# Block attention and a gated MLP on one core: the sums of x's quarters in two places, and all steps in another order

## The chip, the cores and the metric

The kernel runs on one NeuronCore of a Trainium2 chip. The metric is the device time of one execution in microseconds (us); several executions are taken and their median is given. The engines are TensorE (PE, matmuls), VectorE (DVE), ScalarE (ACT), GpSimd (POOL) and SyncE (SP), which here only issues DMA transfers. Each engine works through its own list of instructions in order and waits on semaphores for the others.

## The reference

Eight batches, eight heads, 576 tokens, head size 64. Attention is computed inside chunks of 64 tokens; its output, put together over the heads, is x (8 x 576 x 512), and x goes through a gated MLP:

```python
scores = scale * matmul(q_c, k_c.T);  attn = softmax(scores)      # per chunk of 64 tokens
x = matmul(attn, v_c) put back to [batch, 576, 512]
h = x @ w_in;  h = gelu_tanh(h);  u, v = h[..., :512], h[..., 512:]
v_n = (v - mean) / sqrt(var + 1e-6) * g_ln                          # over the 512 features
v_s = einsum('ts,bsd->btd', w_sg, v_n) + b_sg[None, :, None]        # over the 576 tokens
out = x + (u * v_s) @ w_out
```

All is in float32.

## The kernel before

Everything lies with features on partitions and tokens along the free axis. A product of two float32 matrices is made of three products of their high and low parts (`hi`, `lo`), so PE runs three matmuls for each. From batch 2 on, the products with w_in's half for u and with w_out are not eight quarter products but seven (a Strassen-Winograd scheme, products 1, 5, 2, 6, 3, 7, 4); the sums of weight quarters that it needs (factors) are made once, kept in DRAM and loaded again for every batch into a ring of four places of 512 KB. The sums of x's quarters that products 5, 7, 6 and 4 need are made anew in every batch, by `x_quarters`.

The program is a list of steps. Each step is a generator that issues some instructions and yields; the string `ORDER` (line 53 on) names, token by token, which step issues its next piece, and the loop at the end of the program just follows it. So the order of the instructions on every engine, on SP's queue of transfers too, is written out there. A token is a letter and a number: `v61` is unit 1 of batch 6. The letters that matter here:

- `A`: load of a tile of q, k and v (two tiles make the pair that `P` and `Q` work on; from tile 5 on five transfers each). `S`, `P`: the scores of one or two tiles and their softmax. `T`: transposition of the softmax's result (from tile 5 on DVE transposes blocks, line 556, and ACT copies them, lines 560 and 566). `O`, `Q`: attention output of one or two tiles (line 601) and `keep`, which copies it out of PSUM: the high part xh on ACT (line 629), the low part xl on DVE (631), x itself, xf, on ACT (633), and for the last tokens of a batch two more copies on ACT (640).
- `W`, `w`, `X`, `x`, `Y`: preparation of the weights. `E`, `B`, `C`, `K`: preparation of the factors. `f`: the load of the next factor into the ring (line 311).
- `v`: one of five units of v: 12 matmuls of 128x512 (line 654), gelu on ACT into hs (658), the layer norm's statistics on DVE (662 to 665), a power on POOL (667), the norm on DVE (669), its scaling on ACT (675) and the low part on DVE (677).
- `z`: `x_quarters`, one of four: a sum on POOL (763), its high part by a copy on ACT (766) and its low part on DVE (768), both into xt. `q`: a quarter product of u (781), copied by ACT (790) or added by DVE (793), with a gelu on ACT (795). The results stand in u2, of which there is one tile: a batch's first write to it waits until the tile's last reader of the batch before is done.
- `s`: a unit of the product with w_sg (731). `p`: a quarter product with w_out (849), added up on DVE (854) and stored by SP (860); the stores of products 3, 7 and 4 read u2.

PSUM holds two kinds of buffers: one pair of banks for the scores (`banks`), and three buffers of two banks (`pm`) that all other matmuls take in turn. A buffer comes free when the copy or gelu that reads it last is done. Running quarter products keep a buffer over several steps.

In `x_quarters` before, every sum is written to one place, the quarter (1, 0) of u2:

```python
t = quarter_of(u2[b], 1, 0)
a, c = {5: (x(0, 1), x(0, 0)), 7: (x(1, 1), x(0, 1)), 6: (t, x(0, 0)), 4: (x(1, 0), t)}[p]
X_SUM[p].tensor_tensor(t, a, c, op=ALU.add if p == 6 else ALU.subtract)
```

So a sum waits until DVE has read the one before it for its low part.

Of the kernel before, what the change touches and what calls it, by code (L numbers as in the profile page):

```python
# [74 lines left out]
v24 z24 P16 f6 q22 P14 q26 v24 v24 z24 P14 v24 q23 f7 z24 q26 P14 v24 v24 P14 v24 f8 q23 s20 v24 v24 q22 T15 q23 T14
T15 P16 s21 T15 T15 s20 T15 T15 P16 s20 T14 T14 s20 T14 s20 q27 T14 T14 s21 s21 Q14 f9 q27 P16 q24 A18 s21 P16 Q14 s22
s21 Q14 f10 A19 q27 P16 q24 P16 Q14 s23 s22 T17 s22 s22 T17 T16 T17 s22 T17 s22 T17 T17 s22 p21 T16 s23 T16 s23 s23 p25
s23 f11 T16 s23 s23 p21 p21 p22 f12 s23 T16 T16 p21 p21 p26 f13 p25 p25 p22 P18 p25 p22 f14 p26 p23 P18 P18 p27 f15 p23
P18 v30 p27 p23 f16 P18 p27 P18 P18 p24 v30 v30 Q16 v30 f17 p24 v30 T19 p24 v31 Q16 v30 A20 T18 T19 Q16 v30 T19 T19 v30
# [5 lines left out]
P23 f27 p35 p35 p33 f28 p36 p32 p37 P23 p32 f29 p33 P23 O22 f30 p37 p33 v40 P23 O22 p37 A26 O22 P23 O22 O22 P23 O22 p34
v40 v40 v41 f31 p34 v40 O22 p34 T24 O22 v40 O22 v40 T24 T23 v42 v40 v41 v40 T24 v41 T24 T24 v41 T24 T23 v41 v41 q41 v42
z45 v41 v42 v43 f32 q41 v41 z45 v42 T23 z45 v42 T23 T23 v42 z47 T23 v44 v43 v42 v43 v42 z47 z47 q45 v43 v44 z46 v44 q42
v44 v43 f33 z46 v43 q45 v44 z46 v43 P25 v44 f34 z44 q42 v44 q46 v43 q42 z44 P25 q43 f35 q46 v44 z44 q47 v44 v44 f36 q43
v44 v44 q43 s40 f37 q47 P25 q47 P25 Q23 s40 P25 s40 s41 A27 Q23 P25 s40 Q23 P25 s40 A28 Q23 q44 s41 T26 s41 T25 s42 f38
q44 s41 T26 s41 T26 T26 T26 T26 T25 s43 s42 T25 T25 s42 s42 s42 T25 s42 T25 s42 p41 s43 s43 s43 s43 p45 f39 s43 s43 p41  # L90
p41 P27 s43 f40 p41 p42 p41 p45 p45 P27 p46 f41 p45 p42 p43 f42 p46 p42 P27 p47 f43 p43 P27 p43 v50 p47 f44 P27 p47 P27
P27 p44 v50 v50 Q25 v50 f45 p44 v50 v50 p44 q51 Q25 A29 T27 T28 v50 v51 Q25 T27 T27 v50 T27 f46 Q25 A30 T27 v52 T27 z55
q51 v51 T28 v51 z55 v51 v53 T28 z55 v51 T28 T28 v51 z57 T28 v52 v51 v52 v51 Q27 v53 v52 z57 v53 v52 q55 A31 Q27 z57 v53
z56 Q27 P29 q55 v52 f47 v53 Q27 A32 v53 z56 q52 P29 v53 z56 v52 f48 q52 Q27 q56 z54 Q27 P29 q52 z54 v53 q53 f49 q56 z54
v52 S31 f50 q53 q57 P29 S31 P29 s50 f51 q57 q53 P29 q57 S31 P29 s51 S31 T30 s50 T29 s50 T30 S31 s50 S31 q54 T30 s51 T30
T30 s50 s51 T29 T31 s52 f52 T30 T29 s51 T29 s51 T29 T29 Q29 q54 s52 s53 A33 Q29 s52 s52 Q29 T31 T31 A34 s52 Q29 s52 p51
T31 s52 T31 s53 T31 s53 s53 p55 f53 s53 s53 s53 p51 p51 p52 f54 s53 p51 P32 p51 f55 p55 p55 p52 p56 p55 p52 P32 O31 f56
p53 p56 A35 O31 O31 P32 O31 p57 O31 p53 f57 O31 p53 v60 P32 p57 f58 p57 P32 P32 p54 v60 P32 v60 v61 v60 f59 p54 v60 v60
O31 p54 O31 T33 v60 T32 T33 q61 v60 v61 T33 v61 T33 v62 T33 f60 v61 T33 v61 v61 O31 T32 v61 z65 q61 v61 v63 v62 z65 v62
T32 z65 T32 T32 v62 T32 z67 v64 v63 v63 v62 z67 v62 v63 v62 z67 v63 P34 v64 v63 z66 v64 v63 q65 v62 z66 q62 v64 f61 q65  # L100
z66 v64 v64 z64 q66 f62 q62 v64 v63 q62 q63 v64 f63 v64 q66 P34 v64 Q32 f64 z64 q63 v64 q67 z64 q63 v64 Q32 P34 s60 f65
q67 Q32 q67 Q32 q64 s60 s60 P34 s61 f66 s60 P34 s60 P34 q64 P34 s62 s61 s61 T34 T35 s61 T34 s61 s63 T34 s62 T34 T34 s62
s62 s62 T34 s62 T35 s62 T35 T35 T35 p61 T35 s63 s63 s63 s63 p65 f67 s63 s63 p61 p61 p62 s63 f68 p61 p61 p66 p65 f69 p65
p62 p65 p62 p63 f70 p66 p67 f71 p63 p63 Q34 f72 p67 p67 p64 Q34 Q34 v70 f73 p64 Q34 p64 v71 v70 v70 v70 v70 v70 v72 z75
# [884 lines left out]
```

## Time and profile before

| | |
|---|---|
| time, median of 3 runs | 504.89 us (504.75 to 506.33) |
| the profiled execution | 504.94 us, its span 503.2 us |
| granted clock of PE | 0.999 of full speed over the span |
| busy in the span | PE 483.1 us, DVE 390.4, ACT 342.9, POOL 120.6 |
| instructions | 12519 |

The profile follows one execution. A row of the timeline gives the start in us from the span's start, the duration, the engine, the line of the program, the operation, what it writes and what it reads, the shapes and the count; in brackets stands how long the engine had been idle before it and what ended that. Matmuls overlap, so their ends are modelled.

### The profile page before, as it was taken

What the parts mean: (1) busy time and instruction counts of PE and PEld (TensorE: products, weight loads), DVE (VectorE), ACT (ScalarE), POOL (GpSimd) and SP (SyncE); (2) the same over time, 40 slices, a digit from 0 to 9 for tenths busy, and PEclk for the clock granted to TensorE, in tenths of its full rate; (3) what the DMA queues carried; (4) which work ended last, traced back from release to release, by engine and by line L of the source; (5) the groups of instructions that cost most, each with busy time, mean ns of one, the idle gap of its engine ahead of it and who ended that gap; (6) DMA issues with size and microseconds to landing.
All of it is one profiled execution on the core that took longest, in us unless ns stands there. A gap on an engine that the chain in (4) does not pass through costs nothing.

```text
span 503.2 us, 12519 instructions
## 1 busy us (share of the span) xinstructions
PE 483.1 (96%) x5112; PEld 441.1 (88%) x5112; DVE 390.4 (78%) x678; ACT 342.9 (68%) x645; POOL 120.6 (24%) x106
## 2 busy tenths in 40 slices
PE   3989999999999999999999999999899999999996
PEld 2767899899998789988999889997899889998996
DVE  7888969977855887878769678777859787867555
ACT  5789898833765689659984777649995678625320
POOL 0112000001491351116310362014320260206200
PEclk9999999999999999999999999999999999999999
DMA  8969010387265983897877846487929915192515
GB/s 293 386 181 284 22 44 22 107 246 238 88 229 173 326 258 126 221 292 205 249 214 221 238 136 207 136 295 231 289 70 278 304 63 210 42 326 89 184 57 205
DMA packets 70189, 97.98 MB, mean 195 GB/s; under 512 B 36978, under 2 KB 50290, under 8 KB 70132
## 3 DMA queue, kind: packets, MB, share of 16 engines
q1 hardware_dynamic: 70132, 97.18, 61.5%
q8 instruction: 40, 0.66, 0.5%
q14 instruction: 17, 0.14, 0.1%
HBM read 80.38 MB, written 16.78 MB: 193 GB/s over the span
## 4 chain that ended last, share of the span: by engine, by line
PE 76%; DVE 8%; ACT 7%; DMA 6%; POOL 2%; issue 1%; SPq 0%; POOLq 0%; DVEq 0%; ACTq 0%
PE pm L731 22%; PE pm L654 14%; PE pm L849 11%; PE pm L781 10%; PE pm L703 5%; PE pm L907 4%; PE pm L601 3%; PE banks L502 3%; DMA out_dram<-u 2%; PE pm L246 2%; DMA qkv_t<-qkv 2%; ACT L658 1%; ACT ptT L566 1%; POOL u L763 1%; DMA ring<-factors 1%
## 5 line engine op out<-in xcount | busy, mean ns | idle before, releaser
L731 PE MATMUL pm<-wsg,v 128*128 128x288 f32 x768 | 108.0, 296 | 0.2 <-ACT u L795 0.2
L731 PEld LDWEIGHTS pm<-wsg,v 128*128 128x128 f32 x768 | 103.9, 189 | 0.7 <-ACT u L795 0.3
L539 POOL TENSOR_TENSOR pt<-pt,den 128x1024 f32<-128x1024 f32 (+1 forms) x15 | 27.4, 1825 | 134.0 <-DVE den L536 98.5
L667 POOL TENSOR_TENSOR sm<-sm,neg_half 128x1 f32<-128x1 f32 x36 | 28.5, 794 | 109.0 <-DVE sm L665 107.6
L654 PE MATMUL pm<-wv_h,xl 128*128 128x512 f32 x128 | 51.7, 404 | 2.7 <-DVE xl L631 1.1
L566 ACT COPY ptT<-blocks 32x256 f32<-32x256 f32 x124 | 50.1, 404 | 2.2
L654 PE MATMUL pm<-wv_h,xh 128*128 128x512 f32 x128 | 50.6, 395 | 0.0
L654 PE MATMUL pm<-wv_l,xh 128*128 128x512 f32 x128 | 50.6, 395 | 0.0
L781 PE MATMUL pm<-xt,ring 128*128 128x288 f32 x288 | 44.0, 300 | 1.2 <-ACT xt L766 0.6
L781 PEld LDWEIGHTS pm<-xt,ring 128*128 128x128 f32 x288 | 39.5, 188 | 3.0 <-DVE xt L768 1.3
L849 PE MATMUL pm<-gh,ring 128*128 128x288 f32 x192 | 40.9, 297 | 0.0
L662 DVE BATCH_NORM_STATS2 sm<-hs 128x6 f32<-128x512 f32 x36 | 24.7, 690 | 20.4 <-ACT hs L658 20.2
L781 PE MATMUL pm<-xh,ring 128*128 128x288 f32 x144 | 31.9, 297 | 1.9 <-ACT xf L633 1.2
L654 PEld LDWEIGHTS pm<-wv_h,xl 128*128 128x128 f32 x128 | 24.0, 188 | 9.3 <-DVE xl L631 1.6
L849 PE MATMUL pm<-tv,ring 128*128 128x288 f32 x216 | 31.9, 297 | 0.2 <-DMA ring<-factors 0.2
L677 DVE SCALAR_TENSOR_TENSOR v<-hs,sm,v 128x512 fp32r<-128x512 f32 x32 | 28.1, 881 | 5.0 <-ACT v L675 4.8
L849 PEld LDWEIGHTS pm<-gh,ring 128*128 128x128 f32 x192 | 31.5, 188 | 0.3
L737 DVE TENSOR_TENSOR u<-pm,u 128x576 f32<-128x576 f32 x24 | 18.0, 751 | 17.0 <-PE pm L731 14.2
L849 PEld LDWEIGHTS pm<-tv,ring 128*128 128x128 f32 x216 | 29.7, 188 | 1.1 <-issue 0.6
L654 PEld LDWEIGHTS pm<-wv_h,xh 128*128 128x128 f32 x128 | 24.0, 188 | 5.8
L675 ACT ACTIVATE v<-hs,sm 128x512 fp32r<-128x512 f32 x32 | 22.9, 721 | 8.2 <-DVE hs L669 4.7
L654 PEld LDWEIGHTS pm<-wv_l,xh 128*128 128x128 f32 x128 | 24.1, 188 | 4.8
(175 smaller groups left out, 1151.6 us busy)
## 6 DMA issues: line engine op xcount, KB each, us to landing
ring<-factors SPq DMA_DIRECT2D x84, 512.0 KB, 4.4
qkv_t<-qkv SPq DMA_DIRECT2D x32, 512.0 KB, 5.1
qkv_t<-qkv SPq DMA_DIRECT2D x124, 64.0 KB, 4.3
out_dram<-u SPq DMA_DIRECT2D x18, 288.0 KB, 5.7
factors<-fac SPq DMA_DIRECT2D x16, 256.0 KB, 2.8
out_dram<-ot SPq DMA_DIRECT2D x14, 288.0 KB, 2.3
qkv_t<-qkv SPq DMA_DIRECT2D x3, 768.0 KB, 11.3
wsg<-w_in SPq DMA_DIRECT2D x4, 512.0 KB, 4.0
```

The lines of the kernel that those rows point to most:

```text
L539: eng.tensor_tensor(pt, pt, den.unsqueeze(2).broadcast_to([P, n, D]), op=ALU.mult)
L566: nc.scalar.copy(ptT[q[1 - a], :, a, :], blocks[q[a], :, 1 - a, :])
L654: nc.tensor.matmul(pv, a[:, kt, tok], c[:, kt, :], start=(i == 0), stop=(i == 11))
L662: nc.vector.bn_stats(st, h)
L667: nc.gpsimd.tensor_tensor(rs, rs, neg_half, op=ALU.pow)
L675: nc.scalar.mul(hi, h, rs)
L677: nc.vector.scalar_tensor_tensor(lo, h, rs, hi.bitcast(F32), op0=ALU.mult, op1=ALU.subtract)
L703: nc.tensor.matmul(pm[:, j, :HS], a[:, kt, dc], c[:, kt, j * HS : (j + 1) * HS], start=(i == 0), stop=(i == 11))
L731: nc.tensor.matmul(pm[:, j, :HS], a[:, dc], c[:, m, j * HS : (j + 1) * HS], start=(i == 0), stop=(i == len(ops) - 1))
L781: nc.tensor.matmul(pm[:, e, :HS], a[:, k, e * P : (e + 1) * P], c[:, k, :], start=starts and i == 0, stop=i == len(ops) - 1, skip_group_ch ...
L849: nc.tensor.matmul(pm[:, e, :HS], a[:, k, e * P : (e + 1) * P], c[:, k, :], start=starts and i == 0, stop=i == len(ops) - 1, skip_group_ch ...
L907: nc.tensor.matmul(pm[:, j, :HS], a[:, kt, ec], c[:, kt, j * HS : (j + 1) * HS], start=(i == 0), stop=(i == len(ops) - 1),)
```

## The change

It has two parts. In `x_quarters` the sums stand in two places of u2 by turns: those for products 5 and 6 in the quarter (0, 1), those for 7 and 4 in the quarter (1, 0). The numbers that are summed are the same: 6 is still made from 7's sum, and 4 from 6's.

```diff
         begin_u(b)
-        t = quarter_of(u2[b], 1, 0)
-        a, c = {5: (x(0, 1), x(0, 0)), 7: (x(1, 1), x(0, 1)), 6: (t, x(0, 0)), 4: (x(1, 0), t)}[p]
+
+        t1, t2 = quarter_of(u2[b], 1, 0), quarter_of(u2[b], 0, 1)
+        t, a, c = {
+            5: (t2, x(0, 1), x(0, 0)), 7: (t1, x(1, 1), x(0, 1)), 6: (t2, t1, x(0, 0)), 4: (t1, x(1, 0), t2)
+        }[p]
         X_SUM[p].tensor_tensor(t, a, c, op=ALU.add if p == 6 else ALU.subtract)
```

The other part is the string `ORDER`: the same 1641 tokens, the same steps, in another order over the whole program. Its last line, as an example:

```diff
-f82 p71 p71 p76 f83 p75 p75 p75 p73 p76 p77 p73 p73 p74 p77 p72 p77 p77 p72 p74 p74
+f82 p75 p71 p76 f83 p71 p75 p73 p76 p72 p75 p77 p72 p73 p73 p74 p77 p77 p77 p74 p74
```

Lines after `x_quarters` carry a number higher by three in the changed kernel (763 is 766 there, 781 is 784, 854 is 857). On PE the moves that matter here are these: attention output O0 before the weight steps w2 and w3; in batch 4 O22 behind v41 (it stood before v40); in batch 5 Q27 behind q53 (it stood behind the fourth unit v53, ahead of q52); in batch 6 O31 behind v61 (it stood before the last output products of batch 5); v70 ahead of the last output product of batch 6, p64 (it stood behind it). Three places show what that does to the lists of the other engines.

First, POOL in batch 7 (u_5848 and u_5873 are batch 7's u2, xf is x, line 667 is the power of the layer norm; the brackets name what an instruction waits for). Before:

```order
L667 TENSOR_TENSOR sm<-sm,neg_half 128x1 [waits DVE_49]
L763 TENSOR_TENSOR u_5848<-xf 128x2x288 [waits DMAHW2_49,DMAHW6_49,DMAHW0_49,Activation_49]
L667 TENSOR_TENSOR sm<-sm,neg_half 128x1 [waits DVE_49]
L763 TENSOR_TENSOR u_5848<-xf 128x2x288 [waits DVE_49]
L667 TENSOR_TENSOR sm<-sm,neg_half 128x1 [waits DVE_49]
L763 TENSOR_TENSOR u_5848<-u_5848,xf 128x2x288 [waits DVE_49]
L667 TENSOR_TENSOR sm<-sm,neg_half 128x1 [waits DVE_49]
L763 TENSOR_TENSOR u_5848<-xf,u_5848 128x2x288 [waits DVE_49]
```

and with the change:

```order
L667 TENSOR_TENSOR sm<-sm,neg_half 128x1 [waits DVE_49,Pool_49] x2
L766 TENSOR_TENSOR u_5873<-xf 128x2x288 [waits DMAHW2_49,DMAHW6_49,DMAHW0_49,Activation_49]
L766 TENSOR_TENSOR u_5873<-xf 128x2x288
L667 TENSOR_TENSOR sm<-sm,neg_half 128x1 [waits DVE_49,Pool_49]
L766 TENSOR_TENSOR u_5873<-u_5873,xf 128x2x288 [waits DVE_49,Pool_49]
L667 TENSOR_TENSOR sm<-sm,neg_half 128x1 [waits DVE_49]
L766 TENSOR_TENSOR u_5873<-xf,u_5873 128x2x288 [waits DVE_49,Activation_49,Pool_49]
```

The second sum follows the first with no instruction between and no wait of its own; the third and fourth still wait for DVE.

Second, ACT in batch 6, around the copies of O31 (tile 31 holds the last 64 tokens of batch 6 and the first 64 of batch 7, so `keep` copies it in two parts). Before, with pm_5076 the PSUM buffer of O31, pm_5137 that of v60 and pm_5174 that of v61:

```order
L629 CAST xh_4555<-pm_5076 128x4x64
L633 COPY xf_4554<-pm_5076 128x4x64
L629 CAST xh_5118<-pm_5076 128x4x64
L531 ACT_TABLE_LOAD
L531 ACTIVATE pt_5051<-pt_5051 128x1024
L658 ACT_TABLE_LOAD
L658 ACTIVATE hs_5150<-pm_5137 128x512
L633 COPY xf_5117<-pm_5076 128x4x64
L640 CAST xodd_0_4629<-xh_5118 128x4x64
L675 ACTIVATE v_5200<-hs_5150,sm_5172 128x512
L560 COPY ptT_5199<-blocks_5197 128x512
L658 ACTIVATE hs_5187<-pm_5174 128x512
```

and with the change, with pm_5143 that of v61, pm_5169 that of O31 and pm_5188 that of q61:

```order
L658 ACTIVATE hs_5156<-pm_5143 128x512
L629 CAST xh_4670<-pm_5169 128x4x64
L566 COPY ptT_5166<-blocks_5164 32x8x32 x3
L633 COPY xf_4669<-pm_5169 128x4x64
L629 CAST xh_5233<-pm_5169 128x4x64
L566 COPY ptT_5166<-blocks_5164 32x8x32
L793 COPY u2_5244<-pm_5188 128x2x288
L633 COPY xf_5232<-pm_5169 128x4x64
L640 CAST xodd_0_4737<-xh_5233 128x4x64
L640 CAST xodd_1_4738<-xl_5234 128x4x64
L769 CAST xt_2263<-u2_5244 128x576
L675 ACTIVATE v_5167<-hs_5156,sm_5209 128x512
```

Before, three of O31's six copies stand ahead of v60's gelu, two directly behind it, and one further on; with the change all six stand behind v61's gelu and ahead of v62's, which is the row after those shown.

Third, DVE at the very end of the program, the additions of the last output products (ot is product 2's, the last row is product 4's). Before:

```order
L834 TENSOR_TENSOR tv<-u_5848,tv 128x576
L854 TENSOR_TENSOR u_5848<-pm,xf 128x2x288
L854 TENSOR_TENSOR u_5848<-pm,u_5848 128x2x288
L854 TENSOR_TENSOR u_5848<-pm,kept 128x2x288
L854 TENSOR_TENSOR ot<-pm,kept 128x576
L854 TENSOR_TENSOR u_5848<-pm,xf 128x2x288
L854 TENSOR_TENSOR u_5848<-pm,u_5848 128x2x288
```

and with the change:

```order
L857 TENSOR_TENSOR u_5873<-pm,xf 128x2x288
L857 TENSOR_TENSOR ot<-pm,kept 128x576
L837 TENSOR_TENSOR tv<-u_5873,tv 128x576
L857 TENSOR_TENSOR u_5873<-pm,u_5873 128x2x288
L857 TENSOR_TENSOR u_5873<-pm,kept 128x2x288
L857 TENSOR_TENSOR u_5873<-pm,xf 128x2x288
L857 TENSOR_TENSOR u_5873<-pm,u_5873 128x2x288
```

The addition into ot moved from behind product 7's to ahead of product 3's.

## Rows read from the trace of the kernel before

**Rows 1.** The page, section 1: busy time of each engine, share, instructions.

```profile
PE 483.1 (96%) x5112; PEld 441.1 (88%) x5112; DVE 390.4 (78%) x678; ACT 342.9 (68%) x645; POOL 120.6 (24%) x106
```

**Rows 2.** Timeline of PE, whole span: the longer idle stretches, and what ended each.

```profile
7.72 1.97 PE L493 MATMUL pm<-qkv_t 64*64 64x64 f32 x32 [7.72 <-DMA qkv_t<-qkv]
...
28.93 0.63 PE L549 MATMUL banks<-ident,pt 128*128 128x128 f32 x4 [0.87 <-DVE pt L539]
...
30.23 1.15 PE L582 MATMUL banks<-ptT,qkv_t 64*64 64x64 f32 x32 [0.68 <-ACT xf L622]
...
185.41 0.38 PE L781 MATMUL pm<-xh,ring 128*128 128x288 f32 x1 [0.72 <-ACT u L790]
...
227.09 0.50 PE L654 MATMUL pm<-wv_h,xl 128*128 128x512 f32 x1 [1.12 <-DVE xl L631]
...
280.26 0.50 PE L654 MATMUL pm<-wv_h,xl 128*128 128x512 f32 x1 [0.43 <-ACT hs L658]
...
342.54 0.50 PE L654 MATMUL pm<-wv_h,xl 128*128 128x512 f32 x1 [0.60 <-ACT xf L633]
...
353.60 0.40 PE L781 MATMUL pm<-xh,ring 128*128 128x288 f32 x1 [1.22 <-ACT xf L633]
...
395.87 0.50 PE L654 MATMUL pm<-wv_h,xl 128*128 128x512 f32 x1 [0.43 <-ACT hs L658]
...
465.07 0.40 PE L781 MATMUL pm<-xt,ring 128*128 128x288 f32 x1 [0.57 <-ACT xt L766]
...
465.87 1.73 PE L781 MATMUL pm<-xt,ring 128*128 128x288 f32 x11 [0.39 <-DVE xt L768]
```

**Rows 3.** Timeline of batch 7's sums, all engines, 455 to 468 us.

```profile
455.80 1.68 POOL L763 TENSOR_TENSOR u<-xf 128x576 f32<-128x576 f32 x1 [1.55 <-DMA out_dram<-u]
...
458.22 0.76 DVE L768 TENSOR_TENSOR xt<-u,xt 128x576 fp32r<-128x576 f32 x1 [1.75 <-ACT xt L766]
...
459.06 1.88 POOL L763 TENSOR_TENSOR u<-xf 128x576 f32<-128x576 f32 x1 [1.07 <-DVE xt L768]
...
461.17 1.75 PE L781 MATMUL pm<-xt,ring 128*128 128x288 f32 x12
...
462.89 1.42 POOL L763 TENSOR_TENSOR u<-u,xf 128x576 f32<-128x576 f32 x1 [1.00 <-DVE xt L768]
...
463.34 1.53 DVE L677 SCALAR_TENSOR_TENSOR v<-hs,sm,v 128x512 fp32r<-128x512 f32 x1
```

**Rows 4.** Timeline of DVE's last additions, 495 us to the end.

```profile
497.64 0.75 DVE L854 TENSOR_TENSOR ot<-pm,kept 128x576 f32<-128x576 f32 x1
498.31 0.75 DVE L854 TENSOR_TENSOR u<-pm,xf 128x576 f32<-128x576 f32 x1
...
499.16 0.76 DVE L854 TENSOR_TENSOR u<-pm,u 128x576 f32<-128x576 f32 x1
```

**Rows 5.** Groups of ACT by line and shape: busy us, mean ns | idle before, releasers.

```profile
L566 ACT COPY ptT<-blocks 32x256 f32<-32x256 f32 x124 | 50.1, 404 | 2.2
...
L658 ACT ACTIVATE hs<-pm 128x512 f32<-128x512 f32 x36 | 21.5, 596 | 8.7 <-PE pm L654 6.2 <-issue 1.6 <-DVE v L677 0.7
...
L766 ACT CAST xt<-u 128x576 fp32r<-128x576 f32 x24 | 16.1, 672 | 10.1 <-POOL u L763 9.9
...
L633 ACT COPY xf<-pm 128x256 f32<-128x256 f32 x6 | 2.2, 373 | 5.5 <-DVE u L854 3.2 <-DVE xl L631 2.3
```

**Rows 6.** Timeline of PE, 385 to 404 us: O31, q61, v62, v63 begin.

```profile
386.96 0.69 PE L601 MATMUL pm<-ptT,qkv_t 64*64 64x64 f32 x32
...
398.77 0.30 PE L781 MATMUL pm<-xh,ring 128*128 128x288 f32 x1
...
400.36 0.39 PE L654 MATMUL pm<-wv_h,xl 128*128 128x512 f32 x1
...
403.15 0.40 PE L654 MATMUL pm<-wv_h,xl 128*128 128x512 f32 x1
```

**Rows 7.** Timeline of SP: the first loads into the ring.

```profile
179.50 8.10 SPq L311 DMA_DIRECT2D ring<-factors  x5
```

More of the change, by code (lines that the diff above doesn't have):

```diff
@@ L75 @@
[L75 to L79, printed above, removed]
@@ L85 @@
[L85 to L89, printed above, removed]
@@ L90 @@
[L90 to L104, printed above, removed]
@@ new lines @@
+T14 T14 P16 T14 s21 T14 T15 z24 T15 T15 T15 q23 T15 s20 q27 s20 s21 P16 s21 Q14 f9 q27 s20 P16 s21 q24 A18 Q14 s20 Q14
+s22 f10 q27 P16 s21 A19 P16 Q14 q24 s23 s22 T17 s22 T16 T17 s22 T17 s22 T17 s22 T17 T17 p21 T16 s23 T16 s22 s23 s23 p25
+s23 f11 T16 s23 s23 p21 p21 p22 f12 s23 T16 T16 p21 p26 p21 f13 p25 p25 p22 P18 p25 p22 f14 p26 p23 P18 P18 p27 f15 p23
+P18 v30 f16 p27 p23 P18 p27 P18 P18 p24 v30 v30 Q16 v30 f17 p24 v30 v30 p24 v31 Q16 A20 T19 T18 v30 Q16 T19 T19 v30 T19
+A21 v32 Q16 T18 z35 v31 T19 v31 T19 v33 z37 z35 v31 v32 z35 T18 v31 T18 v31 z37 z36 v32 v31 q31 z37 v33 T18 T18 q35 v31
@@ new lines @@
+T24 p34 v40 T24 T23 v40 O22 T24 v40 v42 T24 A26 O22 v41 O22 T23 v41 O22 O22 v41 T24 O22 v41 T24 q41 v41 O22 O22 z45 O22
+v42 v43 v41 f32 v42 z47 T23 v41 T23 z45 T23 v42 T23 z45 v42 v44 v43 v42 q41 z46 v43 v42 v43 z47 v42 v43 z46 q45 z47 v44
+z46 z44 v43 q42 f33 q45 z44 q46 f34 v44 v43 z44 v43 q43 f35 q46 q42 v44 q42 P25 v44 f36 q43 v44 q43 Q23 P25 v44 q47 v44
+A27 v44 v44 P25 v44 s40 q47 Q23 f37 v44 q47 A28 Q23 P25 q44 s40 Q23 P25 s40 s41 f38 P25 P25 q44 s40 s40 T26 s42 T25 T26
+s41 T26 T26 s41 T26 T26 T25 s41 s43 s42 T25 T25 s41 s42 s42 T25 s42 T25 s42 s42 p41 s43 s43 s43 s43 p45 f39 s43 s43 s43
@@ new lines @@
+p42 p41 p41 f40 p41 p41 p46 f41 p45 p45 p42 P27 p45 f42 p42 p46 p43 P27 P27 p47 f43 p43 P27 v50 p47 p43 f44 P27 p47 P27
+P27 p44 v50 v50 Q25 v50 f45 p44 v50 v50 p44 v51 Q25 A29 T27 T28 v50 Q25 T27 T27 q51 v50 T27 A30 Q25 v51 v52 z55 T27 v51
+T27 f46 T28 v51 z57 z55 q51 z55 v53 v51 v52 v51 z57 z56 v52 T28 v51 z57 T28 q55 T28 v53 v51 z54 T28 v53 z56 q52 v52 f47
+q55 v53 z56 v52 z54 v52 P29 v53 f48 v53 v52 q52 q56 v53 P29 q52 q53 v53 f49 q56 P29 Q27 f50 z54 P29 v52 q57 A31 Q27 q53
+P29 s50 Q27 q53 A32 P29 Q27 q57 P29 Q27 Q27 f51 q57 s51 s50 T30 s50 T29 T30 T29 T30 T30 T30 q54 s51 T30 T29 T29 s51 T29
@@ new lines @@
+S31 T29 f52 q54 Q29 S31 s50 s51 s50 s52 A33 Q29 s51 S31 Q29 A34 S31 s53 s52 s52 s52 S31 Q29 s52 S31 s52 p51 s53 T31 s53
+s53 p55 T31 f53 p51 T31 s53 T31 s53 s53 P32 f54 p55 p51 s53 p52 T31 T31 p51 p51 s52 p56 f55 p52 p55 P32 p52 p53 f56 p56
+p55 p57 f57 p53 P32 p53 v60 f58 p57 P32 p57 P32 p54 v60 P32 P32 v60 v61 v60 f59 p54 v60 v60 p54 T32 v60 O31 T32 v60 q61
+v61 A35 O31 v61 T32 T32 O31 T32 v62 v61 O31 v61 v61 O31 T32 f60 O31 T33 z65 q61 O31 O31 O31 v63 z67 z65 v61 z65 v62 v61
+z67 z66 v62 v64 T33 z67 v63 T33 z66 v62 z64 v63 T33 T33 z66 q65 T33 v62 v64 v62 q62 v64 f61 q65 v63 v62 v64 v63 v63 z64
@@ new lines @@
+q66 f62 q62 v64 v63 v64 q62 P34 v62 f63 q66 z64 v64 q63 v63 v64 v64 v64 P34 q67 f64 v64 v64 s60 q63 f65 q67 q63 P34 q67
+P34 q64 s60 P34 s60 s61 f66 q64 P34 s60 P34 s60 T34 Q32 s61 s62 T35 Q32 s61 T34 Q32 T34 T34 T34 T34 s61 s63 s62 Q32 s61
+s62 s62 T35 s62 s62 T35 T35 T35 s62 T35 p61 s63 s63 s63 s63 p65 f67 s63 s63 s63 p62 p61 p61 f68 p61 p61 p66 f69 p65 p65
+p62 p63 p65 f70 p62 p66 Q34 f71 p63 p63 p67 Q34 Q34 v70 f72 p67 Q34 p67 p64 v70 v70 v71 v70 f73 p64 v70 v70 p64 v70 v70
+v72 v71 v71 v71 v71 v71 v73 v72 z75 v71 v72 v71 z77 z75 v72 z75 q71 v73 v72 z77 v73 q75 z76 f74 q71 v72 z76 q72 f75 v73
```

58 lines of the change are left out of this document (29 added, 29 removed).

## The prediction

> **What bounds the kernel now.** I read the page first. PE is busy 483.1 us, 96% of the span; DVE 78%, ACT 68%, POOL 24% [rows 1]. The change leaves PE's matmuls as they are, so what it can gain is PE's idle time and nothing else, and the next view is PE's own timeline, where every idle stretch ends in a named wait [rows 2]. The first wait, 7.72 us for the first load of q, k and v, stands before any step that the change moves. The ten others shown come to 7.03 us, 0.70 each on average: two at the start (0.87, 0.68), 0.72 in batch 2's first quarter products, then 1.12, 0.43, 0.60, 1.22, 0.43, and two in batch 7 (0.57 and 0.39), where product 6 of u waits for the sum that stands in the shared place. That is 1.4% of the kernel. The reader should see that no single wait is worth 0.3%, so the result is a sum of small terms, and that a reordering wins only if the waits that it takes away do not come back one step later.
>
> The sum is made against the profiled execution, 504.94 us, of which the span is 503.2 and 1.7 lies around it; the median of the runs shown, 504.89, stands 0.05 lower. About 0.3%, 1.5 us, is what a measurement of this kernel can tell from no change.
>
> **The change, part by part.**
>
> *Two places for the sums.* Nothing is added or removed: four sums on POOL, four copies on ACT, four subtractions on DVE per batch, as before. What goes is a wait. In batch 7 the sum for product 7 stood on POOL until DVE had finished product 5's low part, 458.22 plus 0.76, and began at 459.06; the sum for 6 then waited again and began at 462.89 [rows 3]. Product 6's matmuls waited 0.57 and 0.39 for that chain [rows 2]. With two places the sum for 7 stands right behind that for 5 and the one for 6 starts some 1.1 us earlier at least (POOL's wait before 7's, 1.07, is gone [rows 3]). Term: **-0.96**. In batches 2 to 6 the ten waits hold none on these sums, so there it is 0: other products of u, by x's own quarters, cover them.
>
> The first sum of a batch does not move by this: it still waits for the stores of the batch before out of u's memory (1.55 us idle ended by that store's landing [rows 3]). What does move is PE's cover over it. The unit v70 now runs before the last output product of batch 6, so between that product and product 5 of batch 7 there is one v unit less, 2.79 us (403.15 less 400.36 [rows 6]). Product 5 began at 461.17, and its right side was ready at 458.98 [rows 3]: a slack of 2.2. So it should now wait, 0.6 us if nothing else changes, 0.2 if the steps between the last product and the store are issued as tightly as their order now allows. I take **+0.2** (0 to 0.7).
>
> *The start.* The attention output O0 stands before the weight steps w2 and w3 now. The waits at 28.93 and 30.23 (0.87, 0.68) were PE waiting for a softmax on DVE and a copy on ACT that stood behind weight work. Term **-1.55**; what may be left, 0 to 0.3, I take as 0, since PE gets the weight products to run meanwhile.
>
> *Batch 2's first quarter products.* The wait of 0.72 at 185.41 is named after a copy on ACT, but SP's row shows more: the first ring loads left in one run of five from 179.50 on [rows 7], behind the factors' store, and the product took what the last of them brought. The factor's store and this load now come earlier in SP's order: **-0.72**. Close behind, the unit s21's buffer is freed later: DVE's add for q23 stands behind two transposes that wait for a softmax scaled on POOL. Below: 0, if POOL is on time. Above: 1.0, near the longest waits of this kind (1.12, 1.22 [rows 2]). I take **+0.5**, in the middle, since the rows give no nearer one.
>
> *Batch 3.* The 1.12 at 227.09 stays: the same DVE rows stand ahead of the low part it waits for. The 0.60 at 342.54 in batch 5 stays likewise (the buffer's last copy, xf, is where it was).
>
> *Batch 4.* The unit v41's wait (0.43) goes, because O22 with its copies moves behind v41: **-0.43**. In its place the product q42 stands near v44's gelu, whose ACT row waits behind O22's copies and v42's power on POOL: **+0.5** (0 to 0.9).
>
> *Batch 5.* Q27 moves behind q53, so product q52 no longer waits for Q27's last copy: **-1.22**. It now needs the buffer that v53's gelu frees: **+0.3** (0 to 0.4).
>
> *Batch 6.* The same move as in batch 4: O31 behind v61. The wait at 395.87 goes, **-0.43**. The new order on ACT puts O31's copies between the gelus of v61 and v62 (shown ahead of this text). From v61's end PE has O31 0.69, q61 1.59 and v62 2.79 to run, 5.07 us [rows 6]. In that time ACT must run v61's gelu 0.60, four copies of O31 at 0.37, four transposing copies at 0.40 and q61's copy at about 0.63 (a cast of that size takes 0.67): 4.3 us [rows 5]. It begins about 1.2 late, since v60's scaling and a transposing copy stand ahead of v61's gelu. O31's buffer is free at 5.5 or later, and v63 needs it at 5.07: about 0.5 there, 1.0 if a copy waits for DVE between. Behind it stand two more copies, a cast of x's sum and v61's scaling before v62's gelu, about 2.8 us against one v unit of 2.79: 0.2 to 0.5 more at v62 or v64. Together **+1.2** (0 to 1.7).
>
> *The end.* The add that makes ot stood between the last two matmul groups' adds, so DVE reached the very last add only at 499.16, having begun the one before at 498.31 [rows 4]. In the new order ot's add stands three rows earlier; the last add can begin when the last matmul is done, about 0.55 earlier by the 0.75 that ot's add took less the 0.2 DVE then waits: **-0.55** (-0.6 to -0.2).
>
> *Waits that I did not follow.* Every step moved. For the places not worked out (the stretch before batch 2 and s51 with Q29 in batch 5) I add one wait of the mean size of the ten, **+0.7** (0 to 2).
>
> **Sum**: gains -0.96 -1.55 -0.72 -0.43 -1.22 -0.43 -0.55 = -5.86; new waits 0.2 + 0.5 + 0.5 + 0.3 + 1.2 + 0.7 = +3.4. Together -2.5: 504.94 - 2.5 = **502.5 us**. With all new waits at their lower ends the time would be 499.1.
>
> **The rivals.**
>
> *ACT becomes the bound in batches 4 and 6 (slower).* O22's and O31's six copies cost ACT 4 x 0.37 + 2 x 0.40 = 2.3 us [rows 5] each, at the place where PE asks for a freed buffer every 2.8 us. If ACT is already behind when it reaches v61's gelu, none of the 2.3 is absorbed: 4.6 instead of the 1.7 in my sum, +2.9; the gains at v41 and v61 (0.86) come back as the same buffer's wait; s21 at its upper end +0.5. That is 502.5 + 4.3 = 506.8. It decides if O31's last copy ends more than 2 us after v62. For it: both moves are of one kind. Against: ACT is busy only 68% [rows 1]. Chance 0.16.
>
> *The waits come back one for one (no change).* Each step freed runs into the next one's buffer, as three PSUM buffers make likely: 504.9, within 504 to 506. For it: seven of the ten waits are for a copy or gelu on ACT, whose work is the same. Chance 0.24.
>
> *The second place does nothing.* If the sum for 5 comes so late that 7's and 6's are late with it, product 6 still waits 0.96: 502.5 + 0.96 = 503.5. For it: the first sum's wait for the store is untouched. Against: three v units or products lie between. Chance 0.09.
>
> *POOL and DVE exclude each other.* Now POOL runs 7's sum while DVE should subtract product 5's low part, both inputs in SBUF. The nearest rows: two DVE instructions of line 677, with two inputs in SBUF, began at 463.34 inside POOL's sum of 462.89, 1.42 long, and took 1.53 together, 0.77 each, with neither side stretched [rows 3]; but the sum at 459.06 took 1.88. If the subtraction had to wait for the whole sum it would start 1.42 - 0.67 = 0.75 late (0.67 is the cast that overlaps [rows 5]), and so would product 5: 503.3. Chance 0.07. The Trainium skill, "SBUF — State Buffer", section "Who interferes with whom", states just this: a DVE instruction with two SBUF inputs and a GpSimd instruction that reads SBUF take turns, the later one blocked for the whole instruction. By that rule the trace disagrees at 463.34.
>
> **How the numbers follow.** My forecast has 0.44; its own range is 500.2 to 504.5. Faster by over 0.3% means below 503.4: most of the forecast (0.37), half of the third and fourth rivals (0.08), a little of the second (0.03): **0.48**. Slower means above 506.4: the first rival, most of it, and the tail of the second: **0.15**. The rest, **0.37**, is the same. The range that leaves out two in ten goes from 499.9 to 506.4.
>
> **What would show it.** In the changed profile: no PE wait for xt in batch 7's product 6; none before 32 us; POOL's second sum of batch 7 starting without a wait for DVE; v62 to v64 with waits ended by ACT (hs or xf), 1.2 us together; q52 without xf; the last store issued about 0.5 us earlier. PE's idle time between first and last matmul should fall by some 2 us. I am wrong if these waits stay as long in sum, or if batch 6 holds over 2 us.

## The result, and the profile after

The changed kernel took 501.03 us (median of 8 runs, 499.52 to 502.91) where the kernel before took 504.71 beside it (8 runs): a ratio of 0.9919, 95% interval 0.9889 to 0.9948. In a second comparison it took 500.77 against 504.50, 0.9926 (0.9906 to 0.9945). The profiled execution is one of 501.20 us, span 499.4, granted clock 1.0. Compared with the profiled execution of before that is 3.74 us less, and 3.8 in the span.

The page, section 1, of the changed kernel:

```profile
PE 480.9 (96%) x5107; PEld 440.6 (88%) x5112; DVE 393.1 (79%) x678; ACT 339.0 (68%) x643; POOL 118.4 (24%) x106
```

Against [rows 1], PE is busy 2.2 us less with the same 5112 matmuls (a few records are missing), so part of what was gained lay inside rows that the page counts as busy. PE's idle stretches, as in [rows 2]:

```profile
7.16 1.97 PE L493 MATMUL pm<-qkv_t 64*64 64x64 f32 x32 [7.16 <-DMA qkv_t<-qkv]
...
14.54 1.15 PE L493 MATMUL pm<-qkv_t 64*64 64x64 f32 x32 [0.61 <-DMA qkv_t<-qkv]
...
16.95 1.15 PE L582 MATMUL banks<-ptT,qkv_t 64*64 64x64 f32 x32 [0.68 <-ACT ptT L552]
...
24.71 2.05 PE L928 MATMUL pm<-ident 128*128 128x128 f32 x16 [0.75 <-DVE pt L529]
...
36.84 0.66 PE L549 MATMUL banks<-ident,pt 128*128 128x128 f32 x4 [1.14 <-DVE xl L631]
...
38.17 1.15 PE L582 MATMUL banks<-ptT,qkv_u 64*64 64x64 f32 x32 [0.68 <-ACT xf L633]
...
192.03 3.46 PE L731 MATMUL pm<-wsg,v 128*128 128x288 f32 x24 [0.73 <-DVE u L796]
...
228.40 0.50 PE L654 MATMUL pm<-wv_h,xl 128*128 128x512 f32 x1 [1.13 <-DVE xl L631]
...
288.21 0.50 PE L654 MATMUL pm<-wv_h,xl 128*128 128x512 f32 x1 [0.35 <-ACT xf L633]
...
295.98 0.40 PE L784 MATMUL pm<-xh,ring 128*128 128x288 f32 x1 [0.31 <-ACT hs L658]
...
342.83 0.50 PE L654 MATMUL pm<-wv_h,xl 128*128 128x512 f32 x1 [0.59 <-ACT xf L633]
...
401.44 0.50 PE L654 MATMUL pm<-wv_h,xl 128*128 128x512 f32 x1 [0.32 <-ACT xf L633]
```

What answers to [rows 2]: the waits at 185.41, 280.26, 353.60, 395.87, 465.07 and 465.87 are gone, 227.09 and 342.54 stand as they were (228.40, 342.83), and four new ones are here (192.03, 288.21, 295.98, 401.44), 1.71 us together. Ahead of 40 us, where there were two, there are five.

Ahead of s00, and ahead of each batch's first output product (p21, p31, ...), PE has run the same steps in both orders, so the time between these points is a ledger of the change. Windows of the kernel before, which begin at the first matmul, at that of s00, then at p21, p31, p41, p51, p61, p71 (us in the window, then busy time and count of PE, PEld, DVE, ACT and POOL, then the granted clock, DMA's busy share and GB/s):

```profile
7.72:71.02 63.30, 61.75 (x744) 48.16 (x744) 53.79 (x106) 52.77 (x129) 7.21 (x8) 1.00 0.62 201
71.02:206.48 135.46, 134.63 (x1412) 126.17 (x1406) 105.79 (x197) 94.73 (x179) 38.32 (x30) 1.00 0.59 183
206.48:263.17 56.69, 55.57 (x682) 51.90 (x681) 45.79 (x73) 45.29 (x83) 15.75 (x13) 1.00 0.80 234
263.17:320.89 57.72, 56.95 (x567) 52.35 (x565) 46.49 (x76) 40.18 (x69) 15.94 (x13) 1.00 0.64 193
320.89:379.23 58.34, 56.26 (x682) 51.88 (x681) 44.24 (x74) 44.91 (x81) 15.70 (x13) 1.00 0.69 213
379.23:435.78 56.55, 56.12 (x566) 52.13 (x565) 46.26 (x75) 39.00 (x65) 15.39 (x13) 1.00 0.57 182
435.78:487.12 51.34, 50.37 (x394) 47.36 (x393) 32.02 (x52) 19.56 (x32) 11.61 (x10) 1.00 0.50 168
487.12:503.20 16.08, 11.40 (x86) 11.11 (x84) 10.51 (x16) 2.50 (x4) 0.00 (x0) 0.95 0.49 171
```

and of the changed kernel:

```profile
7.16:72.60 65.44, 61.59 (x739) 47.99 (x744) 54.07 (x107) 52.35 (x130) 7.93 (x8) 1.00 0.59 195
72.60:207.78 135.18, 134.45 (x1411) 126.06 (x1405) 105.90 (x198) 94.72 (x179) 36.60 (x30) 1.00 0.60 183
207.78:264.48 56.70, 55.57 (x682) 51.88 (x681) 44.14 (x73) 45.29 (x84) 15.44 (x13) 1.00 0.82 235
264.48:321.18 56.70, 56.04 (x567) 52.06 (x566) 47.47 (x77) 40.05 (x69) 15.28 (x13) 1.00 0.63 196
321.18:377.74 56.56, 55.90 (x683) 52.20 (x682) 44.97 (x71) 42.28 (x77) 15.96 (x13) 1.00 0.78 233
377.74:434.17 56.43, 56.12 (x566) 52.02 (x565) 47.93 (x77) 39.53 (x69) 15.30 (x13) 1.00 0.54 170
434.17:483.94 49.77, 49.77 (x394) 47.27 (x393) 33.41 (x52) 18.60 (x29) 11.23 (x10) 1.00 0.51 173
483.94:499.40 15.46, 11.45 (x86) 11.12 (x84) 10.31 (x16) 2.50 (x4) 0.00 (x0) 1.00 0.54 178
```

Differences, in order: start +2.14; s00 to p21 -0.28; p21 to p31 +0.01; to p41 -1.02; to p51 -1.78; to p61 -0.12; to p71 -1.57; from there to the end -0.62. The first load landed 0.56 earlier (7.16 instead of 7.72; in the other runs it landed at 7.0 to 7.3 with either start, so 7.72 was chance). The sum is -3.80, the spans' difference. **In this pair the start lost 2.1 us; everything behind it gained 5.4.**

From s00 to p71 the changed kernel needs 4.8 us less (411.34 instead of 416.10). Of these, 2.7 come out of PE's idle time (6.20 before, 3.49 after) and 2.1 out of time in which PE counts as busy. Over the whole stretch from the first matmul to p71 the idle time fell by 0.4 us only, 7.75 to 7.34, since the start has more of it.

The end, as in [rows 4]:

```profile
494.38 0.75 DVE L857 TENSOR_TENSOR u<-pm,xf 128x576 f32<-128x576 f32 x1
495.43 0.76 DVE L857 TENSOR_TENSOR u<-pm,u 128x576 f32<-128x576 f32 x1 [0.30 <-PE pm L852]
```

The last addition waits for PE now and not for the one ahead of it.

### The profile page after: what moved, and what is told of

It is laid out like the page before. It is cut to its first block, busy times and chain, and to the rows that moved or that the text cites. A ratio compares the mean times of both kernels' runs of the same rounds, so it can differ in the third digit from the quotient of the medians.

```text
span 499.4 us, 12551 instructions
## 1 busy us (share of the span) xinstructions
PE 480.9 (96%) x5107; PEld 440.6 (88%) x5112; DVE 393.1 (79%) x678; ACT 339.0 (68%) x643; POOL 118.4 (24%) x106
## 4 chain that ended last, share of the span: by engine, by line
PE 79%; ACT 8%; DVE 8%; DMA 3%; issue 1%; SPq 0%; ACTq 0%; DVEq 0%
PE pm L731 23%; PE pm L654 14%; PE pm L852 12%; PE pm L784 11%; PE pm L910 5%; PE pm L703 5%; PE banks L502 3%; PE pm L601 3%; DMA wsg<-w_in 2%; ACT ptT L566 2%; PE pm L246 2%; ACT hs L658 1%; DMA qkv_t<-qkv 1%; ACT L658 1%; DVE blocks L556 1%
## 5 line engine op out<-in xcount | busy, mean ns | idle before, releaser
L539 POOL TENSOR_TENSOR pt<-pt,den 128x1024 f32<-128x1024 f32 (+1 forms) x15 | 26.4, 1760 | 131.8 <-DVE den L536 123.9
L784 PE MATMUL pm<-xt,ring 128*128 128x288 f32 x288 | 42.8, 297 | 0.0
L669 DVE SCALAR_TENSOR_TENSOR hs<-hs,sm,g_bc 128x512 f32<-128x512 f32 x36 | 29.6, 828 | 0.0
L852 PE MATMUL pm<-gl,ring 128*128 128x288 f32 x96 | 28.3, 295 | 0.0
```

Of the source, the lines that this page charges most:

```text
L539: eng.tensor_tensor(pt, pt, den.unsqueeze(2).broadcast_to([P, n, D]), op=ALU.mult)
L669: nc.vector.scalar_tensor_tensor(h, h, mv[:, 0:1], g_bc, op0=ALU.subtract, op1=ALU.mult)
L784: nc.tensor.matmul(pm[:, e, :HS], a[:, k, e * P : (e + 1) * P], c[:, k, :], start=starts and i == 0, stop=i == len(ops) - 1, skip_group_ch ...
L852: nc.tensor.matmul(pm[:, e, :HS], a[:, k, e * P : (e + 1) * P], c[:, k, :], start=starts and i == 0, stop=i == len(ops) - 1, skip_group_ch ...
```

## The experiments

The kernels of these runs are made by writing the order string anew, which takes four lines more: a line is 4 higher than in the kernel it comes from (771 is 775).

### The second place alone

```diff
 ORDER: as before
-        t = quarter_of(u2[b], 1, 0)
+        t1, t2 = quarter_of(u2[b], 1, 0), quarter_of(u2[b], 0, 1)
...
```

> Old order, only the sums in two places. Theory A, that the second place itself shortens the chain of sums: product 6 of u waited for that chain in batch 7 (0.57 + 0.39 us in the trace of before) and, inside rows counted as busy, in batch 4 (a product's 12 matmuls took 2.26 instead of 1.75) and batch 5 (2.11); all three go, 1.7 to 1.8 us, so about 503.0 where before is 504.7. Theory B, that the order of the steps and not the place sets when the sums run: the waits stay, the time is within 0.4 us of before.

The runs were made on three chips, each beside the kernel before; a ratio is to that one, with its 95% interval behind it, and kernels from different chips are best compared by their ratios.

This one took **512.36 us**, 1.0174 (1.0154 to 1.0194) of the kernel before: neither theory, but 8.4 us slower. Timeline of batch 7's sums in this run, all engines:

```profile
463.66 1.43 POOL L770 TENSOR_TENSOR u<-xf 128x576 f32<-128x576 f32 x1
...
463.93 1.78 DVE L775 TENSOR_TENSOR xt<-u,xt 128x576 fp32r<-128x576 f32 x1 [1.76 <-ACT xt L773]
...
472.87 1.72 PE L788 MATMUL pm<-xt,ring 128*128 128x288 f32 x11 [1.71 <-DVE xt L775]
```

Product 7's sum now starts while product 5's low part is due. The low part, begun at 463.93, should take 0.75; it took 1.78 and ended 0.62 after the sum had. The norm and other low parts are stretched likewise. Groups of DVE by line and shape (busy us, mean ns | idle before), of the kernel before, of this run, and of the changed kernel:

```profile
L669 DVE SCALAR_TENSOR_TENSOR hs<-hs,sm,g_bc 128x512 f32<-128x512 f32 x36 | 27.0, 756 | 0.0
...
L768 DVE TENSOR_TENSOR xt<-u,xt 128x576 fp32r<-128x576 f32 x24 | 18.0, 751 | 5.0 <-ACT xt L766 4.9
```

```profile
L673 DVE SCALAR_TENSOR_TENSOR hs<-hs,sm,g_bc 128x512 f32<-128x512 f32 x36 | 33.7, 940 | 0.0
...
L775 DVE TENSOR_TENSOR xt<-u,xt 128x576 fp32r<-128x576 f32 x24 | 23.1, 964 | 5.5 <-ACT xt L773 5.4
```

```profile
L669 DVE SCALAR_TENSOR_TENSOR hs<-hs,sm,g_bc 128x512 f32<-128x512 f32 x36 | 29.6, 828 | 0.0
...
L771 DVE TENSOR_TENSOR xt<-u,xt 128x576 fp32r<-128x576 f32 x24 | 22.4, 942 | 3.4 <-ACT xt L769 3.4
```

In the kernel before, the low part (line 768) takes 751 ns on average, its length alone: the wait on the one place kept every low part out of the way of the next sum. With two places it takes 964 here and 942 in the changed kernel, and the norm (669) 940 and 828 instead of 756. That is the Trainium skill's rule ("SBUF — State Buffer", section "Who interferes with whom"): a DVE instruction with two inputs in SBUF and a GpSimd instruction that reads SBUF exclude each other for the whole instruction. The rows agree with it. The kernel before was not free of it either: its line 677, the low part of v, which also has two inputs in SBUF, took 881 ns on average, 782 in the changed kernel and 747 in the run below with most sums on DVE.

In the old order, product 6 stands so close behind its sum that it waits for the later low part, 1.71 us in batch 3, 1.26 in batch 5 and 1.71 again in batch 7 (the last row of the timeline above; there DVE comes late to the low part, held up by the stretched one before it). That is 4.7 us where the idle column of the kernel before had 0.39. From s00 to p71 this run took 422.4 us instead of 416.1, 6.3 more.

### The changed order with one place

```diff
 ORDER: as changed, but in each batch
-z75 ... z77 ... z75 ... z75 ... z77 ... z76 ... z77
+z75 ... z75 ... z75 z77 ... z77 z77 z76 ...
-        t1, t2 = quarter_of(u2[b], 1, 0), quarter_of(u2[b], 0, 1)
+        t = quarter_of(u2[b], 1, 0)
...
```

> The changed order, but all four sums of a batch in one place again; the sums that would overwrite another too early are held back until the low part before them is made, as in the old order, and nothing else moves. Theory A, that the second place carries part of the gain: product 6 waits again in batches 4, 5 and 7, and the time rises by 1.0 to 1.8 us over the changed kernel, to 502.0 to 502.8. Theory B, that the new order hides the chain without the second place: within 0.4 us of the changed kernel.

**521.43 us**, 1.0346 (1.0324 to 1.0367): far beyond both theories. One place in batch 4 shows how (timeline, all engines):

```profile
303.35 0.67 ACT L770 CAST xt<-u 128x576 fp32r<-128x576 f32 x1 [2.81 <-POOL u L767]
303.93 0.59 ACT L662 ACTIVATE hs<-pm 128x512 f32<-128x512 f32 x1
...
304.57 0.61 PE L785 MATMUL pm<-xh,ring 128*128 128x288 f32 x1 [4.50 <-ACT hs L662]
```

The sums are held back on POOL, but the casts of them keep their place on ACT. ACT stood 2.81 us before such a cast, v44's gelu, which frees a PSUM buffer, stood behind it, and product q42 waited 4.50 us for that buffer. Within this wait PE's granted clock fell, and it was 0.50, the lower of its two levels (1.2 GHz), from 304.5 to 309 us and 1.00 again from 311 to 315, so the wait cost more than its length. The experiment does not price one place by itself, since the steps had to be moved for it; it shows that the changed order is written for sums that come early. In these runs neither part gained alone: 1.0174 and 1.0346 apart, 0.9919 both.

### Is it the exclusion? Sums on DVE

```diff
-X_SUM_ON = {5: "gpsimd", 6: "gpsimd", 7: "gpsimd", 4: "gpsimd"}
+X_SUM_ON = {5: "gpsimd", 6: "vector", 7: "vector", 4: "vector"}
```

This edit was made on the changed kernel, on the old order with two places, and on the kernel before.

> The changed kernel with the sums for products 7, 6 and 4 on VectorE instead of GpSimd (5 stays). Theory A, that VectorE instructions with two inputs in SBUF stand still while GpSimd reads SBUF: the low part (0.94 us on average in the changed kernel, 0.75 before) and the norm (0.83, before 0.76) go back to 0.75, which returns some 6 of the 13.5 us that 18 more sums of 0.75 cost VectorE; the time stays within 1.5 us of 501.0 either way. Theory B, that these instructions take longer for another reason: they stay at 0.9 and 0.8, and the time rises by 2 us or more.

> The old order with two places, as in the run that took 512.4, but with the sums for 7, 6 and 4 on VectorE. Theory A, that the second place in the old order is slow because GpSimd's sum now runs beside VectorE's low part and norm and stops them: those go back to 0.75 us, product 6's waits of 1.7 us in batches 3 and 7 shrink, and the time falls to 503 to 507. Theory B, that two places make the old order late in another way (a wait on ACT, or the sums' order): the time stays above 510.

> The kernel before (old order, one place), with the sums for 7, 6 and 4 on VectorE. On one engine in order the place makes no difference, so this shows what moving the sums costs by itself. Theory A, that the second place in the old order cost nothing but the standstill of VectorE beside GpSimd: this takes the same as old order, two places and sums on VectorE, 509.1, within 0.5%. Theory B, that two places hurt the old order in another way too: it lies near 504.5 to 506, well below 509.1.

On the changed kernel the groups of DVE read:

```profile
L673 DVE SCALAR_TENSOR_TENSOR hs<-hs,sm,g_bc 128x512 f32<-128x512 f32 x36 | 26.5, 744 | 0.0
...
L775 DVE TENSOR_TENSOR xt<-u,xt 128x576 fp32r<-128x576 f32 x24 | 17.8, 748 | 0.6 <-ACT xt L773 0.5
```

Low part and norm are back at 748 and 744 ns: theory A holds for the durations. DVE's busy time is 396.4 us instead of 392.7 in the unedited kernel run beside it, for 18 more sums that take 14.1 us, so some 10 us of standstill went, where 6 were expected. The time did not follow: 502.85 us (0.9970, 0.9951 to 0.9989) against 500.77 (0.9926), outside the 1.5 us given. DVE has the sums to do itself now, and s21 waits 1.56 us for DVE instead of 0.73. The profile is of the fastest execution, 500.58, with a short start; from s00 to p71 it took 412.35 us where the unedited kernel beside it took 411.17.

The old order with two places fell from 512.36 to **509.12** (1.0083, 1.0059 to 1.0106), between the two theories. Its low part is back at 752 ns and its norm at 777:

```profile
L775 DVE TENSOR_TENSOR xt<-u,xt 128x576 fp32r<-128x576 f32 x24 | 18.1, 752 | 5.5 <-ACT xt L773 5.4
```

The waits of product 6 fell from 1.71 to 0.40 in batch 3 and to 0.51 in batch 7. The third run says why it did not fall further: the kernel before with the same edit, where the place makes no difference since one engine does both in order, took 507.64 (1.0066, 1.0048 to 1.0084). So 0.7% is the price of sums on DVE with one place, and with two the ratio is 0.8% with overlapping intervals: without POOL beside it, the second place costs little or nothing even in the old order. The second place thus cost 1.7% beside sums on POOL and 0.2% beside sums on DVE, which supports theory A; the remainder, 1.5 us between the medians on two chips, is not settled. One thing the three runs do not separate: a sum takes 0.75 us on DVE and 1.4 to 1.9 on POOL, so the waits for the sums shrink by that too. The lengths of the low part and the norm show the standstill by itself.

### The start

```diff
 ORDER: the changed kernel with
-its own first 260 tokens
+the first 260 tokens of the order before
```

> The changed kernel, but the first 260 steps of the order (up to the second unit of w_sg's product in batch 0) as before. Theory A, that the new start loses time that nothing behind it gives back: the first unit of w_sg began at 72.60 us instead of 71.02 with the same steps behind it, so the time falls by 1.6 us (2.1 if the first load's landing, 0.56 earlier in the changed profile, was chance) to 499.0 to 499.5 where the changed kernel has 501.0. Theory B, that what stands behind the start waits for loads or factors anyway: the time stays within 0.4 us of the changed kernel.

```diff
 ORDER: the kernel before with
-its own first 260 tokens
+the first 260 tokens of the changed order
```

> The kernel before (one place), but with the first 260 steps in the changed order. Theory A, a lasting loss in the start: 504.7 + 1.6 to 2.1 = 506.3 to 506.8. Theory B: 504.7 within 0.4.

> The changed kernel once more, beside the others, so that the old start can be compared with it on one chip: 501.0 as before. If the start's loss of 1.6 us is real, this lies 1.2 to 2 us above the version with the old start (499.5); if the two agree within 0.4, the start costs nothing.

The old start on the changed kernel took **499.48 us** (498.98 to 499.91), 0.9909 (0.9896 to 0.9922), and the changed kernel again 500.77, 0.9926 (0.9906 to 0.9945). The two were on different chips: against the kernel before beside it, the one is 4.4 us faster and the other 3.7, with overlapping intervals, so the times alone do not show the start's loss. The profiles do: s00 began at 70.67 us instead of 72.60, and p71 at 482.56 instead of 483.94. Of the 1.9 us, 0.55 are given back by p71, partly by a new wait of 0.45 at 134.25. The new start on the kernel before took 507.37, 1.0072 (1.0057 to 1.0087), 3.5 us more than before and more than theory A said. In its profile the clock adds to it: behind the waits of 1.15 and 0.68 that end at 36.60 and 37.93, PE's granted clock was 0.50 from 39 to 41 us, where the changed kernel's profile shows 1.00 behind the same waits, and s00 began 66.94 us after the first matmul. Both runs speak for theory A, the second alone clear of noise.

How much the start costs varies from execution to execution. From the first matmul to s00, the seven profiles with the old start took 63.3 to 64.6 us (median 63.6) and the six with the new one 64.0 to 66.9 (median 65.3): 1.7 us between the medians, 2.1 in the pair above. The last run on the start asks which step it is:

```diff
-... T0 S1 W3 O0 S1 W3 w3 w2 A5 S1 O0 ...
+... T0 S1 W3 S1 W3 w3 w2 O0 A5 S1 O0 ...
```

> The changed kernel with the matmuls of O0 behind the weight step w2, as in the old order; nothing else moves. Theory A, that the start lost its time because O0 stands right behind T0, whose copy on ACT it needs (0.68 us wait at 16.95 in the changed profile), and each later step is that much late: 500.9 less 0.7 and more. Theory B, that the later waits of the start (0.75, 1.14 and 0.68, for softmax, low part and copy of other tiles) take the time back: within 0.3 of 500.9.

**499.96 us** (498.73 to 505.29, a wide spread; 0.9927, 0.9905 to 0.9949). In ratio that is the changed kernel's 0.9926, so the time shows no gain. In the one profile s00 began at 70.79 and p71 at 482.43. PE's waits of its start:

```profile
20.84 0.63 PE L553 MATMUL banks<-ident,pt 128*128 128x128 f32 x4 [0.23 <-ACT xodd L644]
...
23.44 2.05 PE L932 MATMUL pm<-ident 128*128 128x128 f32 x16 [0.43 <-DVE pt L533]
...
35.02 0.66 PE L553 MATMUL banks<-ident,pt 128*128 128x128 f32 x4 [0.19 <-DVE xl L635]
...
36.35 1.15 PE L586 MATMUL banks<-ptT,qkv_u 64*64 64x64 f32 x32 [0.68 <-ACT xf L637]
```

Against the changed kernel (0.68, 0.75, 1.14, 0.68 from O0 on), the 0.68 for O0 is gone, 0.75 became 0.43 and 1.14 became 0.19, and 0.23 is new. From the first matmul to s00 it took 63.65 us, as with the old start. But the run above with the sums on DVE has the changed start untouched and took 63.95, with no wait of 0.75 and with 0.24 in place of 1.14. So only the 0.68, which stands in all six profiles of the new start (0.67 in one), is shown to be O0's; that O0 makes the waits behind it too, as theory A has it, is not shown.

### Q27 back ahead of product 5

```diff
-... z57 T28 q55 T28 v53 v51 z54 T28 v53 z56 q52 ... q56 P29 Q27 f50 ...
+... z57 T28 T28 T28 Q27 v53 q55 Q27 v51 Q27 z54 v53 z56 Q27 q52 ... q56 P29 f50 ...
```

> The changed kernel with the attention output Q27 (its matmuls and the copies up to xf) ahead of product 5 of batch 5 again, as in the old order, with T28's copies and v53's gelu ahead of it. Theory A, that its move behind q53 is what took away q52's wait for xf: the wait of about 1.2 us comes back and the time rises by 0.8 to 1.5 us over 500.9. Theory B, that other parts of the new order made it: no wait for xf, the time within 0.4 of 500.9.

**504.48 us**, 1.0006 (0.9990 to 1.0023). Two waits of PE in batch 5:

```profile
350.25 1.16 PE L605 MATMUL pm<-ptT,qkv_t 64*64 64x64 f32 x62 [1.55 <-ACT ptT L570]
...
354.83 0.40 PE L788 MATMUL pm<-xh,ring 128*128 128x288 f32 x1 [1.64 <-ACT xf L637]
```

The wait of q52 for xf is back, 1.64, which is theory A. The other, 1.55, is the experiment's own: Q27 stands close behind the copies of T28 there. The rise, 3.7 us where 0.8 to 1.5 were expected, is mostly the two (3.2 together), so the run shows the mechanism, not its price alone.

### Two attempts at a better version

```diff
 ORDER: first 480 tokens as before, the rest as changed, two places
-... q26 T14 z24 T15 T14 q23 ...
+... q26 q23 T14 z24 T15 T14 ...
-... Q16 A20 T19 T18 v30 Q16 ...
+... Q16 A20 Q16 T19 T18 v30 ...
```

> Two places; the first 480 steps in the old order, the rest in the changed one, with two pieces moved: the add of product 3 in batch 2 ahead of the two transpositions on VectorE behind which it stood (s21 waited 0.73 for it), and the low part of Q16 ahead of the transpositions of tiles 19 and 18 (v32 waited 1.12 for it, in both kernels). Theory A, that these waits are lasting: 499.5 - 0.73 - 1.12 - 0.3 = 497.3. Theory B, that PE meets the same time again at the next buffer: 499.5.

**500.55 us** (0.9917, 0.9896 to 0.9938), no faster than the old start alone (499.48, 0.9909): theory B. The waits of 0.73 and 1.12 are gone and 0.57, 0.17, 0.57, 0.30 and 0.45 stand behind them, one for a factor's load.

```diff
 ORDER: first 480 tokens as before, the rest as changed, two places
-... T19 A21 v32 Q16 T18 ... v33 ... v31 q31 z37 ...
+... T19 A21 q31 v32 Q16 T18 ... v33 ... v31 z37 ...
```

> Two places, the first 480 steps in the old order, the rest in the changed one, and in batch 3 the first quarter product q31 ahead of v32 instead of behind v33, so that PE has 1.6 us of work while VectorE makes the low part of Q16 that v32 waited 1.12 us for. Nothing moves on the other engines. Theory A, the wait is covered: 499.5 less 1.1, and 0.3 for a small wait that goes with the first 480 steps: 498.1. Theory B, that q31 holds a PSUM buffer from there on and the v units wait for one instead: 499.2 to 499.8.

**500.05 us** (0.9918, 0.9902 to 0.9934). v32's wait became 0.59, now for xf of Q16, which frees a buffer: nearer to theory B. The best version measured is the changed kernel with the old start, 499.48; its interval overlaps with the others'.

## Why the prediction was right, and where it was wrong

The forecast, 502.5 and faster, was right in direction and range, -2.5 forecast and -3.7 measured between the profiled executions. But two large errors of opposite sign stand inside it, and that they partly cancel is luck: with the rest as forecast, the start as measured would have given about 506 us. The premise that PE's idle time is all that can be gained failed as well: behind the start 2.1 us came out of rows counted as busy, and of the signs named, "none before 32 us" and idle time lower by some 2 us did not show (three waits, 0.4 us).

- **The start, -1.55 forecast, +2.1 measured (1.7 between the medians of the profiles).** The step that failed is "PE gets the weight products to run meanwhile". O0 was moved ahead of w2, so it stands right behind T0 and PE waits 0.68 for ACT's copy of it; steps behind it wait too, 1.14 at 36.84 and 0.68 at 38.17. I had looked at which waits the old places caused, not at what the new place asks for. The loss is shown by the old start put back, in its profile, and by the new start put on the old kernel; O0 alone is shown to make the 0.68, and what makes the rest stays open.
- **The two places, -0.96.** The wait in batch 7 went as forecast. "In batches 2 to 6 there it is 0" was wrong: in batches 4 and 5 a low part also held PE inside rows counted as busy, where PE's idle column shows nothing. Twelve such matmuls usually take 1.75 us; in the kernel before, these two rows took 2.26 and 2.11, and the weight loads inside them (PEld) show the wait (timelines of PE and PEld):

```profile
297.68 2.26 PE L781 MATMUL pm<-xt,ring 128*128 128x288 f32 x12
...
298.21 1.50 PEld L781 LDWEIGHTS pm<-xt,ring 128*128 128x128 f32 x11 [0.34 <-DVE xt L768]
...
355.27 2.11 PE L781 MATMUL pm<-xt,ring 128*128 128x288 f32 x12
...
355.67 1.48 PEld L781 LDWEIGHTS pm<-xt,ring 128*128 128x128 f32 x11 [0.34 <-DVE xt L768]
```

  They are gone in the changed kernel, with some 0.9 us. From p61 to p71, 0.6 us more than the named waits went from PE's time (51.34 us with 0.97 idle became 49.77 with none).
- **The fourth rival, POOL and DVE in turns, 0.07.** It is what happens. The step that failed is the reading of a row: I took the one at 463.34 in [rows 3] for two instructions of 0.77; its count is x1. It is one, stretched to 1.53 beside POOL's sum, and it spoke for the rule. So did the sum's 1.88 at 459.06: DVE's norm had begun at 458.89, and POOL's sum then took 0.45 more than its 1.43. The profile after shows product 5's low part stretched as the rival said, and the norm too (timeline of batch 7, all engines):

```profile
455.16 3.32 POOL L766 TENSOR_TENSOR u<-xf 128x576 f32<-128x576 f32 x2
...
457.38 1.71 DVE L771 TENSOR_TENSOR xt<-u,xt 128x576 fp32r<-128x576 f32 x1
...
459.47 1.42 POOL L766 TENSOR_TENSOR u<-u,xf 128x576 f32<-128x576 f32 x1
...
459.62 1.82 DVE L669 SCALAR_TENSOR_TENSOR hs<-hs,sm,g_bc 128x512 f32<-128x512 f32 x1
```

  In batch 7 it cost PE nothing: product 5 did not wait, so the new order covers the 0.75 that the rival charged. In the old order it is the likeliest cause of most of the 8 us.
- **Batch 2.** -0.72 forecast and found; the new wait of s21 0.73, for 0.5. Right.
- **Batch 4.** v41's 0.43 went. New waits 0.31 at q42 as forecast (0 to 0.9) and 0.35 at a v unit for O22's xf, which I had only under batch 6. 
- **Batch 5.** q52's 1.22 went, and nothing took its place (0.3 forecast). Right, with the mechanism shown by the run that put Q27 back.
- **Batch 6.** +1.2 forecast, 0.32 measured. O31's buffer came free at 401.39, 5.5 us after v61's end as worked out. The second part (0.2 to 0.5 at v62 or v64, and 1.0 for a copy that waits for DVE) did not happen; the term was put at its pessimistic end, and its "about 2.8 us" before v62's gelu is 2.2 by the four rows named (0.41, 0.40, 0.67, 0.72 in the changed kernel's timeline). The slower rival hung on the same mechanism and fell with it.
- **Product 5 of batch 7**, +0.2 forecast, 0 found. **The end**, -0.55 forecast, -0.62 measured.
- **+0.7 for waits not followed**: behind the start there was none of that size.

Without the start, the forecast was -0.9 and the kernel gave -5.4 from s00 on. The waits that went (0.72, 0.43, 1.22, 0.43, 0.96) are 3.8, the new ones 1.7 where I had put 3.4, the end gave 0.6, the two stretched rows 0.9 and the rows counted as busy from p61 to p71 0.6: 4.2 in all. The other 1.2 us are spread over small waits and rows counted as busy and are not traced to single rows.
